# 138 unread bfloat16 products on TensorE in the first part of an attention and two-MLP kernel

## The chip, the cores and the metric

The kernel runs on one core of one Trainium2 chip. The metric is the time of one execution in device microseconds; lower is better. A profile is one execution recorded by the hardware profiler: every instruction with its engine, start and duration, and what it waited for. The engines are TensorE (PE, and PEld for its weight loads), VectorE (DVE), ScalarE (ACT), GpSimd (POOL) and SyncE (SP, whose queue issues the loads). [...]

## The reference

All inputs are float32 tensors in the reference; q, k and v have 4 sequences, 8 heads, 576 positions and 64 features. The weights come to the kernel as 64-bit floats.

```
scores = q @ k.T / 8, masked: heads 0-3 see 32 positions back,
         heads 4-7 see every 4th position up to 128 back
x = softmax(scores) @ v                      # -> 2304 tokens x 512
xn = x / rms(x) * rms_g
x = (silu(xn @ w_gate) * (xn @ w_val)) @ w_out    # d_ff 1536
h = x @ w_in2
out = (max(h, 0) + alpha * min(h, 0)) @ w_out2    # d_ff 2048
```

## The kernel before

The kernel keeps all weights in on-chip memory (SBUF), in 70 slots of 128 x 512 words. A weight block is 512 KB of 64-bit floats; there are 36 blocks of the first MLP (12 each of gate, value and output weights, in chunks of 3 and 9 columns of blocks) and 32 of the second. `load_w` (line 205) loads a block on the SP queue. `decode_w` (line 221) turns it, or a pair of blocks, into float32 by three integer instructions on VectorE (lines 231 to 233). `gram_w1` (line 286) multiplies each decoded gate and value block with itself, four bfloat16 products of 128 x 128 that add into a tile of the pool `ps_a` (tag `acc`, three buffers); once a chunk is complete, VectorE reduces the sums (line 298), `over_partitions` (line 327) spreads the result over the partitions with one product against ones (line 333), and `root_scale` makes the scales. Only then can `split_w` (line 400) cut a block of that chunk into two float16 halves (ScalarE at line 404, VectorE at line 409 or ScalarE and GpSimd at 406 and 407). The first chunk hangs on the first 6 blocks, the second on all 24 gate and value blocks.

The attention works in groups of up to 128 queries. Each of the first groups goes through `f_turn` (q and k are transposed on TensorE, line 639, and ScalarE copies them to a slot, line 642), `f_score` (mask products, then float32 score products of 64 rows; VectorE takes the maximum, line 578; ScalarE the exponentials, line 585), `f_turn_p` (line 670), `f_value` and, for every second group at first, a normalization (`a_norm`, line 734; its rows are transposed at line 750). Groups 0 to 3 make the rows of token block 0. The steps stand in a list; each is wrapped in `early`, which puts its instructions 400 places ahead in the order of priority. Between the steps `pump_to` decodes blocks: 8 of them over the first 18 steps, then more. A planner orders each engine's instructions by these priorities and its own estimate of when each is ready; each engine then takes its instructions in that order.

Behind that come the two MLPs by token blocks of 256 or 384 columns: `mm1` (gate and value), `mm2` (output, into `acc` tiles), `mm3` and `mm4` the same for the second MLP. All products of `mm` are at line 97. `ones_1` is a constant tile of ones in bfloat16, set by VectorE at line 136; `head(b)` is the upper bfloat16 half of a decoded block.

Of the kernel before, what the change touches and what calls it, by code (L numbers as in the profile page):

```python
# [8 lines left out]
F32 = mybir.dt.float32  # L9
F16 = mybir.dt.float16  # L10
BF16 = mybir.dt.bfloat16
# [18 lines left out]
def kernel(  # L30
# [19 lines left out]
    KD = DM // 128  # L50
# [14 lines left out]
    ps_a = ps_stack.enter_context(tc.tile_pool(name="ps_a", bufs=3, space=PSUM))  # L65
# [12 lines left out]
    ones_1 = const.tile([128, 128], BF16, name="ones_1")  # L78
# [17 lines left out]
    def mm(o, a, b, start, stop):  # L96
        nc.tensor.matmul(o, a, b, start=start, stop=stop)  # L97

    def psw():
        return ps_w.tile([128, 512], F32, tag="w", name="psw")  # L100
# [7 lines left out]
    def b_o(c):  # L108
        return 3 * c + 2
# [128 lines left out]
    def dec(b):  # L238
        d = dec_at[b]
        return wb[:, d * 512:(d + 1) * 512]  # L240

    def head(b):
        d = dec_at[b]
        return wbb[:, d * 1024:(d + 1) * 1024].rearrange("p (k f t) -> p k f t", f=128, t=2)[:, :, :, 1]
# [15 lines left out]
    def chunk(c):  # L260
        return max(i for i in range(NCH) if ch0[i] <= c)
# [11 lines left out]
    def gram(blocks, sums, dst):  # L273

        g = psw()
        last = len(blocks) - 1
        for n, b in enumerate(blocks):
            for kc in range(KD):
                w = head(b)[:, kc, :]
                if sums:  # L280
                    mm(g[:, 0:128], w, w, n + kc == 0, n == last and kc == KD - 1)
                else:
                    mm(g[:, n * 128:(n + 1) * 128], w, w, kc == 0, kc == KD - 1)
        nc.vector.tensor_reduce(dst, g[:, 0:128 if sums else (last + 1) * 128], axis=AX.X, op=ALU.max)  # L284

    gsum = {}

# [16 lines left out]
    def norm_w(b):  # L304
        if b < NW1:
            ch = chunk(b // 3)
            if b % 3 < 2:
                gram_w1(b)
            elif b == b_o(ch0[ch + 1] - 1):
                gram([b_o(c) for c in range(ch0[ch], ch0[ch + 1])], True, sqo[:, ch:ch + 1])  # L310
        else:

            n, p = (b - NW1) // 2, (b - NW1) % 2
            junk = wk.tile([128, 512], BF16, tag="junk", bufs=1, name="junk")
            nc.scalar.activation(junk, dec(b), ACTF.Square, accum_out=sq2[:, p, n:n + 1])
            if b == NBLK - 1:
                g = psw()
                sb = const.tile([128, 2], F32, name="sb")
                nc.vector.tensor_reduce(sb, sq2, axis=AX.X, op=ALU.add)
                mm(g[:, 0:2], ones_1, eps[:, 0:2], True, False)  # L320
                mm(g[:, 0:2], ones_1, sb.bitcast(BF16).rearrange("p (n t) -> p n t", t=2)[:, :, 1], False, True)
                nc.vector.tensor_copy(sb2, g[:, 0:2])
# [118 lines left out]
    groups = []  # L441
# [177 lines left out]
    def drop(g, name):  # L619
        for i in g["slots"].pop(name):  # L620
            give(i)
# [9 lines left out]
    def f_turn(i):  # L631
        g = groups[i]
        nq, nk = g["nq"], g["nk"]
        ps = psw().rearrange("p (a c) -> p a c", c=128)
        qk = f32_slot(g, "qk").rearrange("p (a c) -> p a c", c=128)
        g["qk"] = qk
        for u, m in ((0, nq), (1, nk)):
            for a in range(2):
                nc.tensor.transpose(  # L639
                    ps[:, 2 * u + a, :m], g["rqk"][:m, u, 2 * a:2 * a + 2, :].rearrange("p h d -> p (h d)"), ident[:m, :m])  # L640
        if nq == nk:
            nc.scalar.activation(qk[:, :, :nq], ps[:, :, :nq], ACTF.Copy)
        else:
            nc.scalar.activation(qk[:, 0:2, :nq], ps[:, 0:2, :nq], ACTF.Copy)
            nc.scalar.activation(qk[:, 2:4, :nk], ps[:, 2:4, :nk], ACTF.Copy)
        drop(g, "rqk")
# [155 lines left out]

    def turn(i):
        f_turn(i)
        if i >= 3:
            next_load(i)

# [91 lines left out]
    acc = {}  # L899
# [300 lines left out]
    n_done = [0]  # L1200
# [6 lines left out]
    def pump(n):  # L1207

        for _ in range(n):
            if made or loaded:  # L1210
                if made:
                    b = made.popleft()
                else:
                    b = loaded.popleft()

                    if loaded and n_done[0] >= ALONE and abs(raw_at[b] - raw_at[loaded[0]]) == 2 and can_load():
                        pairs[0] += 1
                        made.append(loaded.popleft())
                    decode_w(b, *made)
                norm_w(b)  # L1220
                n_done[0] += 1
                if b == b_o(C1 - 1):
                    scale_wo()
                if b == NBLK - 1:
                    scale_w2()
            fill()
# [32 lines left out]
    fill()  # L1259
    nc.sync.dma_start(out=al, in_=alpha.rearrange("(c p) -> p c", p=128))  # L1260
    constants()

    first = max(n for n, s in enumerate(steps) if s[1] == 0) + 1
    for n in range(first):
# [7 lines left out]
    for s in slots:  # L1272
        kind, j, c = s
# [42 lines left out]
    for n in range(len(order) + 1):  # L1316
        if n < len(order):
            t, cp = order[n]
# [8 lines left out]
        while behind and (n == len(order) or len(behind) > LAGT + (behind[0][1] == 0 < behind[0][0])):  # L1327
            t, cp = behind.popleft()
# [39 lines left out]
```

## Time and profile before

| | |
|---|---|
| three runs | 954.87, 955.4 and 956.1 us; median 955.4 us |
| profiled execution | span 953.2 us from its first to its last instruction; no other time is given for it |
| instructions | 18826, of which TensorE 6760 products |
| TensorE busy | 907.5 us (95%) |
| VectorE busy | 624.7 us (66%) |
| ScalarE busy | 549.1 us (58%) |
| GpSimd busy | 319.1 us (33%) |
| mean granted clock | 0.981 |

Busy time is the time in which at least one instruction of the engine runs. A wait is put down to the instruction that released it. Times in the rows are microseconds from the start of the span.

### The profile page before, as it was taken

Reading aid. Unit: us, or ns where it says so; the run is one execution under the profiler, and the core shown is the slowest. Engines: PE = TensorE matmul, PEld = TensorE weight load, DVE = VectorE, ACT = ScalarE, POOL = GpSimd, SP = SyncE. Lnnn points to the kernel's source line nnn. Section 1 sums busy time; section 2 is a strip of 40 time slices with the busy share of each in tenths; the row PEclk is TensorE's granted clock in tenths of the full one; section 3 lists DMA queues with packets and bytes.
Section 4 is the critical chain, followed back from the end, with each engine's and each line's share of the span. In section 5 each row is a group of like instructions: output and inputs, shape, how many; then the busy total and the mean of one; then the engine's idle time right before and its main releaser. Section 6 shows DMA issues by size and latency. Waiting matters only on the chain.

```text
span 953.2 us, 18826 instructions
## 1 busy us (share of the span) xinstructions
PE 907.5 (95%) x6760; PEld 621.2 (65%) x6760; DVE 624.7 (66%) x1569; ACT 549.1 (58%) x1541; POOL 319.1 (33%) x324
## 2 busy tenths in 40 slices
PE   6668799999999999999999999999999999999997
PEld 4656676775556676555555555555775558889986
DVE  4999997999777555554664765344545837576564
ACT  3436587766799967767665777544524324443342
POOL 2222441131345544332433233232252622322221
PEclk9678999999999999999999999999999999999999
DMA  9992446555435554544454653322301001000000
GB/s 252 327 353 89 120 132 187 144 159 138 86 70 107 97 108 74 123 86 100 102 88 74 114 105 70 65 64 42 55 14 23 1 1 35 1 24 17 9 24 23
DMA packets 191613, 88.14 MB, mean 92 GB/s; under 512 B 176800, under 2 KB 180384, under 8 KB 191520
## 3 DMA queue, kind: packets, MB, share of 16 engines
q1 hardware_dynamic: 189504, 83.27, 37.8%
q10 hardware_dynamic: 2016, 3.67, 1.1%
q8 instruction: 53, 0.87, 0.4%
q14 instruction: 40, 0.33, 0.1%
HBM read 55.32 MB, written 6.55 MB: 65 GB/s over the span
## 4 chain that ended last, share of the span: by engine, by line
PE 83%; DVE 9%; DMA 3%; issue 2%; ACT 1%; SPq 1%; POOL 0%; DVEq 0%; ACTq 0%; POOLq 0%
PE psw L97 41%; PE acc L97 24%; PE p L97 16%; DVE wb L232 2%; DVE wb L233 1%; DVE wb L231 1%; DVE wb L409 1%; DMA wb<-in_moe_w_out_dram 1%; PE psw L670 1%; PE psw L639 1%; SPq L629 1%; DMA wb<-in_q_dram 1%; DVE t L921 1%; DVE t L922 0%; DMA rkv<-in_k_dram 0%
## 5 line engine op out<-in xcount | busy, mean ns | idle before, releaser
L97 PEld LDWEIGHTS <-wb 128*128 128x128 f16 (+1 forms) x4866 | 452.3, 98 | 196.1 <-DVE wb L233 16.7
L97 PE MATMUL psw<-xyall,wb 128*128 128x384 f16 (+1 forms) x2784 | 425.2, 303 | 2.8 <-DVE sqo L284 1.2
L97 PE MATMUL acc<-wb,hlall 128*128 128x512 f16 x822 | 197.6, 379 | 0.2 <-POOL hlall L930 0.2
L97 PEld LDWEIGHTS <-hlall 128*128 128x128 f16 x822 | 79.4, 98 | 79.8 <-POOL hlall L930 0.7
L930 POOL TENSOR_TENSOR hlall<-t,hlall 128x384 f16<-128x384 f32 (+1 forms) x58 | 58.4, 1006 | 150.0 <-ACT hlall L924 132.2
L97 PE MATMUL acc<-wb 128*128 128x512 f16 (+1 forms) x402 | 83.3, 354 | 13.9 <-DVE wb L233 13.9
L97 PE MATMUL p<-xyall,wb 128*128 128x256 f16 (+1 forms) x960 | 88.7, 251 | 0.0
L1098 POOL TENSOR_TENSOR wb<-fa,wb 128x640 f16<-128x640 f32 x32 | 45.4, 1420 | 112.0 <-ACT wb L1097 108.2
L97 PE MATMUL p<-wb 128*128 128x256 f16 x672 | 77.6, 273 | 0.0
L920 ACT ACTIVATE t<-psw,tsc 128x384 f32<-128x384 f32 (+1 forms) x84 | 44.1, 525 | 55.4 <-PE psw L97 54.3
L921 DVE SCALAR_TENSOR_TENSOR t<-t,psw 128x384 f32<-128x384 f32 (+1 forms) x84 | 41.0, 489 | 48.0 <-ACT t L920 48.0
L589 ACT ACTIVATE s<-s,mx 96x128 f32<-96x128 f32 (+2 forms) x132 | 50.1, 380 | 20.9 <-DVE mx L581 20.1
L404 ACT ACTIVATE wb<-wb,wsg 128x512 f16<-128x512 f32 x68 | 46.3, 711 | 16.9 <-DVE wsg L341 10.2
L705 POOL TENSOR_TENSOR phl<-s,phl 96x512 f16<-96x512 f32 (+2 forms) x33 | 35.8, 1084 | 58.2 <-ACT phl L699 41.0
L930 POOL TENSOR_TENSOR hlall<-p,hlall 128x256 f16<-128x256 f32 (+1 forms) x49 | 39.3, 803 | 44.5 <-ACT hlall L987 41.3
L985 DVE SCALAR_TENSOR_TENSOR p<-m,oma,psw 128x256 f32<-128x256 f32 (+1 forms) x64 | 34.7, 542 | 26.7 <-ACT m L984 25.4
L407 POOL TENSOR_TENSOR wb<-wb 128x512 f16<-128x512 f32 x28 | 37.3, 1337 | 41.6 <-ACT wb L406 15.8
L930 POOL TENSOR_TENSOR wb<-t,wb 128x256 f16<-128x256 f32 (+1 forms) x26 | 27.2, 1046 | 70.3 <-ACT wb L924 70.3
L233 DVE SCALAR_TENSOR_TENSOR wb<-wb 128x512 int32<-128x512 int32 (+1 forms) x56 | 49.7, 890 | 0.3
L924 ACT ACTIVATE hlall<-t 128x384 f16<-128x384 f32 (+1 forms) x58 | 27.7, 477 | 37.8 <-DVE t L922 37.8
L737 POOL TENSOR_TENSOR ms<-ms,mhalf 96x1 f32<-96x1 f32 (+2 forms) x24 | 17.2, 718 | 96.2 <-DVE ms L736 84.5
L922 DVE SCALAR_TENSOR_TENSOR t<-t,psw 128x384 f32<-128x384 f32 (+1 forms) x84 | 41.0, 488 | 11.4 <-PE psw L97 10.1
(203 smaller groups left out, 1317.0 us busy)
## 6 DMA issues: line engine op xcount, KB each, us to landing
wb<-in_moe_w_out_dram SPq DMA_DIRECT2D x28, 512.0 KB, 4.6
wb<-in_moe_w_in_dram SPq DMA_DIRECT2D x16, 512.0 KB, 3.8
wb<-in_moe_w_gate_dram SPq DMA_DIRECT2D x12, 512.0 KB, 6.7
wb<-in_moe_w_val_dram SPq DMA_DIRECT2D x12, 512.0 KB, 6.7
out_dram<-o ACTq DMA_DIRECT2D x14, 256.0 KB, 2.7
rkv<-in_k_dram SPq DMA_DIRECT2D x23, 128.0 KB, 2.6
rkv<-in_v_dram SPq DMA_DIRECT2D x23, 128.0 KB, 2.7
rq<-in_q_dram SPq DMA_DIRECT2D x23, 96.0 KB, 2.2
```

What stands on the lines that cost most here:

```text
L97: nc.tensor.matmul(o, a, b, start=start, stop=stop)
L233: nc.vector.scalar_tensor_tensor(w, r[:, :, :, 0], 29, w, ALU.logical_shift_right, ALU.bitwise_or)
L404: nc.scalar.activation(half(b, 0), dec(b), ACTF.Copy, scale=wsg[:, s:s + 1])
L407: nc.gpsimd.tensor_tensor(half(b, 1), dec(b), half(b, 0), ALU.subtract)
L589: nc.scalar.activation(s[:nq, h, :nk], s[:nq, h, :nk], ACTF.Exp, bias=mx[:nq, 1, h:h + 1], scale=-1.0, accum_out=g["dn"][:nq, h])
L705: nc.gpsimd.tensor_tensor(phl[:nq, 1, :, :nk], g["s"][:nq, :, :nk], phl[:nq, 0, :, :nk], ALU.subtract)
L920: nc.scalar.activation(t[:, :T], pg[:, :T], ACTF.Tanh, scale=tsc[:, chunk(c):chunk(c) + 1])
L921: nc.vector.scalar_tensor_tensor(t[:, :T], t[:, :T], 1.0, pg[:, :T], ALU.add, ALU.mult)
L922: nc.vector.scalar_tensor_tensor(t[:, :T], t[:, :T], 2.0 ** -46, pv[:, :T], ALU.mult, ALU.mult)
L930: nc.gpsimd.tensor_tensor(a[:, 1, :T], t[:, :T], a[:, 0, :T], ALU.subtract)
L985: nc.vector.scalar_tensor_tensor(p[:, :T], m[:, :T], oma[:, c:c + 1], ps[:, :T], ALU.mult, ALU.add)
L1098: nc.gpsimd.tensor_tensor(l[:, 3:8], f[:, 3:8], h[:, 3:8], ALU.subtract)
```

## The change

Three places get products whose results nobody reads. All write one tile `hot` of 128 x 512 float32, which is taken from the pool `ps_a` ahead of all its other tiles. The moving operand is always `ones_1`, read four times over (512 columns); the stationary one is `ones_1` itself (10 products, behind the constants and ahead of the first step), the upper bfloat16 half of q and k as `f_turn` left them (8 products in each of turns 0 to 3), or the four parts of a decoded block (4 products for each of the first 24 decoded blocks, behind its Gram products).

```diff
+    HEAT, HEATED = 10, 24
+    hot = ps_a.tile([128, 4, 128], F32, tag="acc", name="hot")
+
+    def heat(w):
+
+        mm(hot, w, ones_1.unsqueeze(1).to_broadcast([128, 4, 128]), True, True)
+
     gsum = {}
...
     def turn(i):
         f_turn(i)
+        if i < 4:
+            qk = groups[i]["qk"].rearrange("p a c -> p (a c)").bitcast(BF16).rearrange("p (a c t) -> p a c t", a=4, t=2)
+            for n in range(8):
+                heat(qk[:, n % 4, :, 1])
         if i >= 3:
             next_load(i)
...
                 norm_w(b)
+                for kc in range(KD if n_done[0] < HEATED else 0):
+                    heat(head(b)[:, kc, :])
                 n_done[0] += 1
...
     constants()
+    for _ in range(HEAT):
+        heat(ones_1)
```

## Rows read from the trace of the kernel before

**Rows 1.** The page: busy tenths of two engines and granted clock, 40 equal slices.

```profile
PE   6668799999999999999999999999999999999997
DVE  4999997999777555554664765344545837576564
PEclk9678999999999999999999999999999999999999
```

**Rows 2.** Engines by stage: length, busy us and instructions of each engine, clock, DMA.

```profile
5.43:14.65 9.22, 5.78 (x25) 3.00 (x25) 4.82 (x9) 1.79 (x3) 2.19 (x6) 1.00 1.16 283
14.65:31.40 16.75, 16.72 (x89) 13.62 (x88) 12.48 (x42) 8.56 (x37) 0.00 (x0) 1.00 1.05 283
31.40:50.40 19.00, 11.36 (x62) 9.83 (x62) 18.68 (x36) 8.74 (x16) 7.65 (x4) 0.55 1.01 342
50.40:64.00 13.60, 10.82 (x100) 8.97 (x100) 13.60 (x23) 4.06 (x13) 1.55 (x1) 1.00 1.03 411
64.00:77.70 13.70, 6.24 (x44) 4.77 (x42) 12.63 (x29) 4.00 (x13) 2.14 (x2) 0.50 0.67 208
77.70:104.20 26.50, 23.28 (x207) 19.90 (x205) 26.46 (x45) 18.15 (x47) 10.56 (x8) 1.00 0.33 99
104.20:117.00 12.80, 8.03 (x74) 6.91 (x74) 11.53 (x23) 7.77 (x17) 7.08 (x7) 0.87 0.32 101
```

**Rows 3.** Mask products by shape, in 14:24 and 50.5:63.5: busy us, mean ns, idle before.

```profile
L97 PE MATMUL psw<-m_spp,ident 128*128 128x256 bf16 x4 | 1.6, 412 | 0.0
L97 PE MATMUL psw<-m_spp,ident 128*128 128x256 bf16 x2 | 0.6, 278 | 0.0
```

**Rows 4.** TensorE's timeline: start, duration, instruction and count, idle before and its releaser.

```profile
4.58 0.28 PE L97 MATMUL psw<-et 4*128 4x128 bf16 x1 [4.58 <-POOL et L149]
5.43 1.30 PE L639 MATMUL psw<-ident,wb 128*128 128x128 f32 x4 [0.57 <-DMA wb<-in_q_dram]
...
12.12 0.61 PE L97 MATMUL acc<-wb 128*128 128x128 bf16 x4 [0.26 <-DVE wb L233]
...
29.84 0.41 PE L97 MATMUL acc<-wb 128*128 128x128 bf16 x4
...
63.78 0.88 PE L97 MATMUL acc<-wb 128*128 128x128 bf16 x8 [2.14 <-DVE wb L233]
70.69 1.89 PE L97 MATMUL acc<-wb 128*128 128x128 bf16 x16 [6.03 <-DVE wb L233]
74.01 0.39 PE L97 MATMUL psw<-diag,ones 128*128 128x256 bf16 x1 [1.43 <-DVE diag L331]
...
74.41 0.64 PE L97 MATMUL psw<-m_spp,ident 128*128 128x256 bf16 x2
74.84 0.42 PE L97 MATMUL psw<-m_spd,ident 128*128 128x256 bf16 x1
...
82.62 0.62 PE L97 MATMUL psw<-wb 128*128 128x128 bf16 x8 [1.69 <-ACT wb L585]
```

**Rows 5.** TensorE in stretches of 0.1 us: length, busy us, clock, DMA.

```profile
63.90:64.00 0.10, 0.10 (x4) 0.95 0.91 369
...
77.60:77.70 0.10, 0.10 (x2) 0.79 0.00 0
```

**Rows 6.** TensorE's timeline, products of 512 columns.

```profile
135.62 5.99 PE L97 MATMUL acc<-wb 128*128 128x512 f16 x27
```

**Rows 7.** VectorE's waits in 0:110: total us, times, longest.

```profile
DVE mx L578 <- PE psw L97: 3.6, 5, 1.3
```

**Rows 8.** VectorE's timeline, columns as in rows 4.

```profile
15.91 0.76 DVE L578 TENSOR_REDUCE mx<-psw 128x2 f32<-128x256 f32 x2 [1.04 <-PE psw L97]
...
25.37 0.40 DVE L231 TENSOR_SCALAR wb<-wb 128x512 int32<-128x512 int32 x1
...
73.03 0.41 DVE L298 TENSOR_REDUCE tmp<-acc 128x2 f32<-128x256 f32 x1
```

**Rows 9.** The SP queue's timeline: issue of block 4's load.

```profile
18.11 0.42 SPq L212 DMA_DIRECT2D wb<-in_moe_w_gate_dram  x1
```

**Rows 10.** DMA issues in 0:80: count, KB each, median us to landing.

```profile
wb<-in_moe_w_gate_dram SPq DMA_DIRECT2D x12, 512.0 KB, 6.7
```

## The prediction, made before the change was run

> **What bounds the kernel now.** I read the 40 slices of the page first, then the engines by stage, then the timelines of TensorE and VectorE in the first 120 us, because all 138 added products lie there. The slices [rows 1] show TensorE at nine tenths or more from the sixth slice (119 us) to the end, and short of it only before, while VectorE is full from the second slice on. By stage [rows 2], VectorE is busy 12.48 of 16.75 us in 14.65 to 31.40, then 18.68 of 19.00, 13.60 of 13.60, 12.63 of 13.70, 26.46 of 26.50 and 11.53 of 12.80. So up to 117 us VectorE (decoding the weights, splitting them, the attention's small steps) is the limit, and TensorE waits for it; behind that TensorE has work without a gap. The work behind 117 us is not touched. The end therefore moves by what the change does to VectorE's idle time before 117 us, or to TensorE's stalls just ahead of that point, and by nothing else.
>
> The clock is the second thing to see. [...] Two such products back to back take 0.64 us where one takes 0.42 [rows 4], so 0.22 us for each further 256 columns, which makes an estimate of 0.43 us for 512 columns. Four Gram products took 0.61 us at 12.12 and 0.41 us at 29.84 [rows 4], so the rise came between; the granted clock later falls at 33.3, rises at 50.4, falls at 64.0, rises at 77.7 and falls again at 108.3 (two of the five shown [rows 5]). At the high level 27 products of 512 columns took 5.99 us, 0.22 us each [rows 6].
>
> **The change part by part.** It removes nothing, adds no DMA and no instruction on any engine but TensorE: 138 products with their weight loads, 10 + 4 x 8 + 24 x 4. At 0.22 us that is 30.4 us, at 0.43 us 59.3 us. Their tile takes one of the three buffers that the accumulators rotate through. The first block's two accumulators then meet it and that of the first chunk's Gram sums, both long done; I cost that at nothing. The slots of turned q and k and of decoded blocks get one more reader, in each case ahead of or beside readers that they have already: nothing, too.
>
> *Ten products ahead of all else.* They need only a constant that VectorE sets at about 1.1 us. TensorE's first product starts at 4.58 us and its first transpose at 5.43 [rows 4]. Ten at 0.43 us end at about 5.4. Cost 0, covered by the wait for the first q and k; without that cover 4.3 us.
>
> *Twenty-four products of turns 0 to 2 and eight of blocks 0 and 1, in 5.43 to 14.65.* At the high level 32 x 0.22 = 7.0 us. TensorE is idle there for 9.22 - 5.78 = 3.44 us [rows 2], and its 5.78 busy us, now at the low level, would give back half, 2.9. The first score comes 0.7 us late.
>
> *From the first score to the last, 14.65 to 24.8.* All of it is at the low level; at the high one it gives back half of 10.2 us, 5.1. The eight products of turn 3 cost 1.8 us. The eight of blocks 2 and 3 would cost 1.8 more if they stood ahead of the scores. The attention's steps are put 400 places ahead in the planner's order and the pump's products are not, so I let those eight fall behind. The last score then ends 0.7 + 1.8 - 5.1 = 2.6 us earlier (0.8 with the eight ahead). VectorE's five waits for score products sum to 3.6 us [rows 7], one of 1.04 us ahead of the first maximum, which stays [rows 8]. What is left, 2.6 us, is as much as the scores gain: I take -2.6. Its bounds are 0 and all 4.27 idle us of that stretch [rows 2]. VectorE can't use the time for decoding, since block 4 is decoded only at 25.37 us [rows 8] and its load takes 6.7 us from an issue at 18.11 [rows 9, 10]; it can use it for the attention steps that now lie behind that point.
>
> *Blocks 4 to 19, 31 to 64 us.* VectorE's waits for TensorE hardly occur here. TensorE is idle 7.64 and 2.78 us in the two stretches from 31.40 to 64.00 [rows 2], and most of the first is at the low level. About 56 products at 0.22 us (12.3 us) fit into 10.4 idle us and some 5 given back. Cost 0; without this cover, 2.
>
> *Blocks 20 to 23, from 70.69.* Here the products are in the way. TensorE waits until 70.69 for the last decoded blocks, makes 16 Gram products in 1.89 us, and VectorE reduces them at 73.03; one product at 74.01 spreads the result, and the scales of the remaining 18 gate and value blocks hang on it [rows 4, 8]. Twelve added products stand ahead of the last block's Gram. At the high level these are 2.6 us, and the Gram products give back 0.9: they end at 74.3 rather than 72.6, where VectorE is ready at 73.03. That is 1.3 us late, of which I let other decoding cover half: +0.7. At the low level (1.89 + 12 x 0.43, ending at 77.7) it is 4.7; with a rise in the middle about 3. I take the high level, because the added products of blocks 16 to 21 shorten the pause ahead of them, but the rows speak against it nearly as much: the clock fell at 64.0 after a pause of 2.14 us [rows 4, 5]. [...]
>
> *74 to 77.7.* Now at the low level throughout; the products before raise the clock sooner. Half of 3.7 us is 1.8, of which ScalarE's exponentials, whose wait stops TensorE for 1.69 us ahead of 82.62 [rows 4], pass on about -1.0 (0 to -1.8).
>
> *104 to 117.* TensorE idles 4.77 us [rows 2] for VectorE's normalized rows and runs slowly from 108.4 on; no added product is left by then: 0.
>
> Sum: -2.6 + 0.7 - 1.0 = -2.9 us. The profiled span is 953.2 us and the median of the runs 955.4, so 2.2 us lie outside the span; the span becomes 950.3 and the time **952.5 us**.
>
> **The rivals.**
>
> *Slower: the products run at the low level ahead of the first score.* Before 29.8 us even gap-free work stayed slow [rows 2, 3], so dense products may stay slow too. Then 32 x 0.43 = 13.8 us meet 3.44 idle us, and the first score, and all behind it, comes 10.3 us late; VectorE waits for it, less about 3 us of its idle time that decoding takes up: 955.4 + 7 = **962.4**. It decides from about 0.3 us a product on, where the delay of the first score eats what the scores give back. Against it: the slow stretch is made of products that use 64 rows or f32 operands, and no row shows bfloat16 products of 128 rows and 512 columns. Chance 0.20.
>
> *No change: the clock falls in the pause before the last four blocks.* TensorE has no more products from block 19's to the decoding of the last blocks, up to 4 us. Falling as at 64.0 [rows 5], it begins the 16 Gram and 12 added products slowly, +3.0 in place of +0.7, and the -1.0 is kept: **954.8**. Chance 0.19.
>
> *No change: VectorE's waits stay.* The exponentials on ScalarE and block 4's arrival set the pace before 25 us, the freed time goes to waiting for them, and the first term is 0: 955.4 + 0.7 - 1.0 = **955.1**. For it: transfers from 2 to 60 us leave the queues hardly a gap. Against it: the waits name the score products [rows 7]. Chance 0.12.
>
> *Much faster: the stall ahead of 117 us goes as well.* The second four attention groups come early by as much as the first, and the 4.77 us of idle time with 1.7 us of low clock vanish: 952.5 - 6.5 = **946.0**. Against it: VectorE is full from 77.7 to 104.2 [rows 2], so those steps have no room to move in. Chance 0.13.
>
> **How the numbers follow.** The forecast has 0.36. A change of 0.2%, 1.9 us, is about what a measurement of this kernel can tell from none. Faster: forecast, last rival and a little of the falling clock, 0.51. Same: most of the two in the middle, 0.22. Slower: the first rival, and 0.07 of the others, since a planner that gets 138 more instructions may order other work worse; 0.27. The forecast's own range is 950 to 953.5. To leave out no more than 0.2 the range reaches to 945.5 (the stall gone) and to 961.5, just short of the full price of the slow products, of which half is thus held.
>
> **What would show it.** Right: mask products at 14 to 24 us at 278 ns, not 412; VectorE's waits for scores near 1 us in sum; the first score within 1 us of 14.65; the last decoded block's reduction at 71 to 72 us, not 73.03; VectorE without gaps up to a point 2 to 4 us earlier. Wrong: added products at 0.43 us behind 6 us; the product of 74.01 later than now; another order of VectorE's decoding with new waits. The forecast fails if the clock is not raised by the first ten, or if other work waits in TensorE's queue behind products that nobody reads.

## The result and the profile after

The changed kernel took 961.71 us (median of four runs, 960.6 to 964.44), the kernel before beside it 955.75 (954.87 to 957.1): a ratio of 1.0065, 95% interval 1.0045 to 1.0084. It is about 6 us slower. The forecast was 952.5, faster; the time lies just above the range, which ends at 961.5. The profiled execution took 961.12 us with a span of 958.9, against 953.2 before, so 5.7 us are to be found.

First the page of the changed kernel, the busy tenths and the granted clock (the profile's share of full speed that TensorE was given, in tenths) in 40 slices, as in [rows 1].

```profile
PE   8898699999999999999999999999999999999997
DVE  4999987999777655654656665344455736666564
PEclk9989799999999999999999999999999999999999
```

TensorE is fuller in the first four slices (8898, 6668 before), and the low clock of the second to the fourth is nearly gone (989, 678 before). In the fifth slice, from 96 to 120 us, both fell: TensorE from 7 to 6, the clock from 9 to 7. VectorE's digits differ little; the stages, with the bounds and columns of [rows 2], say where it lost.

```profile
5.43:14.65 9.22, 7.78 (x45) 4.12 (x45) 4.87 (x9) 1.80 (x3) 2.15 (x7) 1.00 1.18 292
14.65:31.40 16.75, 16.75 (x117) 11.19 (x116) 10.45 (x38) 8.58 (x37) 0.00 (x0) 1.00 1.06 277
31.40:50.40 19.00, 14.85 (x100) 9.53 (x99) 18.69 (x40) 8.46 (x17) 4.57 (x4) 0.91 0.98 327
50.40:64.00 13.60, 11.22 (x67) 7.39 (x66) 12.66 (x17) 3.01 (x12) 0.93 (x1) 0.75 0.99 387
64.00:77.70 13.70, 12.89 (x99) 7.77 (x98) 12.49 (x23) 2.76 (x11) 2.94 (x2) 1.00 0.67 216
...
104.20:117.00 12.80, 4.44 (x27) 3.56 (x25) 12.80 (x22) 6.87 (x14) 6.27 (x7) 0.65 0.38 111
```

VectorE's busy time fell from 12.48 to 10.45 us in 14.65 to 31.40 and from 13.60 to 12.66 in 50.40 to 64.00. TensorE now has no idle time at all in the first of these. Its timeline, with the columns of [rows 4], shows what fills it.

```profile
1.20 4.45 PE L97 MATMUL hot<-ones 128*128 128x512 bf16 x10 [1.20 <-DVE ones L136]
...
7.11 1.90 PE L97 MATMUL hot<-ones,wb 128*128 128x512 bf16 x8
...
13.17 2.76 PE L97 MATMUL hot<-ones,wb 128*128 128x512 bf16 x12 [0.46 <-ACT wb L649]
15.77 0.27 PE L646 MATMUL psw<-ident,wb 128*128 128x128 f32 x1
15.88 0.27 PE L97 MATMUL psw<-m_spp,ident 128*128 128x256 bf16 x1
...
16.30 0.72 PE L97 MATMUL psw<-wb 64*128 64x128 f32 x8
...
21.50 1.90 PE L97 MATMUL hot<-ones,wb 128*128 128x512 bf16 x8
...
26.21 0.49 PE L97 MATMUL psw<-wb 64*128 64x128 f32 x2
...
73.92 0.40 PE L97 MATMUL acc<-wb 128*128 128x128 bf16 x4 [0.81 <-DVE wb L233]
74.16 1.02 PE L97 MATMUL hot<-ones,wb 128*128 128x512 bf16 x4
...
77.21 0.39 PE L97 MATMUL acc<-wb 128*128 128x128 bf16 x4
...
110.33 1.08 PE L757 MATMUL psw<-ident,wb 128*128 128x128 f32 x4 [4.77 <-DVE wb L745]
115.00 1.11 PE L757 MATMUL psw<-ident,wb 128*128 128x128 f32 x4 [3.59 <-DVE wb L745]
```

The clock did rise: a group of eight products takes 1.90 us from 7.11 on, and a mask product 0.27 us at 15.88, where it took 412 ns [rows 3]. The granted clock does not show this: it reads 1.00 from 5.43 to 31.40 us in both kernels. But twelve unread products stand directly ahead of the last transposes and of the first score (13.17), and sixteen more between the first score and the last, eight of them in one row (21.50). The first score starts at 16.30, 1.65 us later than before, and the last one ends at 26.70, where it ended at 24.85. The same places in the kernel before, with the transposes of the two normalized rows at 106 and 109 us:

```profile
14.65 1.23 PE L97 MATMUL psw<-wb 64*128 64x128 f32 x8
...
23.63 1.22 PE L97 MATMUL psw<-wb 64*128 64x128 f32 x4
...
106.10 0.63 PE L750 MATMUL psw<-ident,wb 128*128 128x128 f32 x4 [1.91 <-DVE wb L738]
108.76 1.09 PE L750 MATMUL psw<-ident,wb 128*128 128x128 f32 x4 [2.03 <-DVE wb L738]
```

VectorE's waits in 0 to 110 us (columns of [rows 7]) and its timeline show who pays.

```profile
DVE mx L585 <- PE psw L97: 7.6, 7, 2.5
DVE tmp L305 <- PE acc L97: 0.8, 1, 0.8
```

```profile
17.04 0.76 DVE L585 TENSOR_REDUCE mx<-psw 128x2 f32<-128x256 f32 x2 [2.47 <-PE psw L97]
...
24.19 0.43 DVE L585 TENSOR_REDUCE mx<-psw 128x2 f32<-128x256 f32 x1 [1.87 <-PE psw L97]
...
60.62 0.42 DVE L585 TENSOR_REDUCE mx<-psw 128x2 f32<-128x256 f32 x1 [0.94 <-PE psw L97]
...
77.64 0.43 DVE L305 TENSOR_REDUCE tmp<-acc 128x2 f32<-128x256 f32 x1 [0.77 <-PE acc L97]
```

The waits for scores are 7.6 us in seven places; they were 3.6 in five [rows 7]. The reduction of the second chunk's Gram sums is at 77.64 instead of 73.03 [rows 8]. That reduction is the first of three points between which the 5.7 us can be divided, by the VectorE timelines of both kernels:

| from | to | before | after | difference |
|---|---|---|---|---|
| start | reduction of the second chunk | 73.03 | 77.64 | +4.61 |
| that reduction | second normalized row behind it (L738, now L745) | 34.84 | 35.92 | +1.08 |
| that row | reduction of the square sums (L284) | 8.08 | 8.79 | +0.71 |
| that reduction | end of the span | 837.25 | 836.55 | -0.70 |

Of the first 4.61 us, 3.90 are idle time of VectorE (16.99 us ahead of the reduction, 13.09 before). The remaining 0.7 is not more work: the same 131 instructions stand ahead of it in both kernels, and they take 60.65 us instead of 59.93. In the second line VectorE has other work: 69 instructions instead of 64, busy 1.6 us longer and idle 0.5 us less. The five stand behind the row in the kernel before. The third line has a longer low clock in it: the clock fell at 108.1 us (108.4 before), but in 1-us stretches (columns of [rows 2]) it is low until 118.3 us, where it was low until 111.8 before.

```profile
108.00:109.00 1.00, 0.00 (x0) 0.00 (x0) 1.00 (x1) 0.33 (x2) 0.10 (x1) 0.54 0.00 0
...
118.00:119.00 1.00, 1.00 (x10) 0.82 (x8) 0.85 (x2) 0.00 (x0) 0.00 (x0) 0.84 1.00 227
```

### The profile page after: what moved, and what is told of

Read it like the earlier page. It is cut to its first block, busy times and chain, and to the rows that moved or that the text cites. A ratio compares the mean times of both kernels' runs of the same rounds, so it can differ in the third digit from the quotient of the medians.

```text
span 958.9 us, 19102 instructions
## 1 busy us (share of the span) xinstructions
PE 927.3 (97%) x6898; PEld 624.9 (65%) x6898; DVE 626.4 (65%) x1569; ACT 548.5 (57%) x1541; POOL 316.3 (33%) x324
## 4 chain that ended last, share of the span: by engine, by line
PE 78%; DVE 9%; issue 4%; ACT 4%; DMA 3%; POOL 1%; SPq 0%; DVEq 0%; POOLq 0%; ACTq 0%
PE psw L97 36%; PE acc L97 22%; PE p L97 16%; PE hot L97 2%; DVE wb L232 1%; ACT wb L411 1%; DVE wb L233 1%; DMA wb<-in_moe_w_out_dram 1%; DVE wb L231 1%; DVE wb L416 1%; PE psw L646 1%; ACT s L596 1%; DVE t L933 1%; DMA rkv<-in_k_dram 1%; ACT wb L413 1%
## 5 line engine op out<-in xcount | busy, mean ns | idle before, releaser
L97 PEld LDWEIGHTS <-wb 128*128 128x128 f16 (+1 forms) x4994 | 462.4, 98 | 202.1 <-DVE wb L233 10.4
L932 DVE SCALAR_TENSOR_TENSOR t<-t,psw 128x384 f32<-128x384 f32 (+1 forms) x84 | 41.1, 489 | 48.4 <-ACT t L931 48.3
L996 DVE SCALAR_TENSOR_TENSOR p<-m,oma,psw 128x256 f32<-128x256 f32 (+1 forms) x64 | 34.7, 542 | 26.7 <-ACT m L995 25.3
L233 DVE SCALAR_TENSOR_TENSOR wb<-wb 128x512 int32<-128x512 int32 (+1 forms) x56 | 48.7, 873 | 0.3
L232 DVE SCALAR_TENSOR_TENSOR wb<-wb 128x512 int32<-128x512 int32 (+1 forms) x56 | 48.6, 872 | 0.2
```

The source lines that it names most:

```text
L232: nc.vector.scalar_tensor_tensor(w, r[:, :, :, 1], -0x40000000, w, ALU.bitwise_and, ALU.bitwise_or)
L233: nc.vector.scalar_tensor_tensor(w, r[:, :, :, 0], 29, w, ALU.logical_shift_right, ALU.bitwise_or)
L932: nc.vector.scalar_tensor_tensor(t[:, :T], t[:, :T], 1.0, pg[:, :T], ALU.add, ALU.mult)
L996: nc.vector.scalar_tensor_tensor(p[:, :T], m[:, :T], oma[:, c:c + 1], ps[:, :T], ALU.mult, ALU.add)
```

## The experiments

Three theories stood when they began. **Theory A, the queue:** score and Gram products that VectorE waits for stand behind products that nobody reads, as the first score at 16.30 does behind the twelve of 13.17; what a place costs depends on who waits there, and grows with the columns. **Theory B, the thing itself:** the tile that takes a turn among three buffers, or the earlier rise and later fall of the clock, costs the time wherever the products are. **Theory C, the order:** 138 more instructions lead the planner to another order of VectorE's work, and that order is worse whatever TensorE does.

All edits are against the changed kernel; all ratios are against the kernel before, timed on the same chip. The table has, from the profiled run of each, VectorE's idle time ahead of the second chunk's reduction, the start of that reduction, the time from it to the second normalized row behind it, the start of the square sums' reduction, and the span.

| run | unread products | ratio, 95% interval | idle | reduction | to row | squares | span |
|---|---|---|---|---|---|---|---|
| before | 0 | 1 | 13.09 | 73.03 | 34.84 | 115.95 | 953.2 |
| after | 138 | 1.0065, 1.0045 to 1.0084 | 16.99 | 77.64 | 35.92 | 122.35 | 958.9 |
| e1_first10 | 10 | 0.9992, 0.9976 to 1.0008 | 13.37 | 73.39 | 34.85 | 116.27 | 953.0 |
| e4_one | 1 | 0.9994, 0.9979 to 1.0009 | 13.60 | 73.69 | 34.85 | 116.65 | 955.2 |
| e2_first_and_turns | 10 + 32 | 1.0002, 0.9984 to 1.0020 | 14.05 | 74.18 | 34.71 | 118.44 | 956.7 |
| e16_first_two | 10 + 16 | 1.0000, 0.9987 to 1.0014 | 11.59 | 71.51 | 35.15 | 116.56 | 953.2 |
| e13_narrow_turns | 10 + 32 narrow | 1.0081, 1.0057 to 1.0105 | 14.26 | 74.93 | 35.29 | 119.24 | 955.9 |
| e23_first_eight | 10 + 32 at blocks 0 to 7 | 1.0020, 1.0006 to 1.0034 | 14.83 | 75.31 | 34.85 | 119.25 | 955.6 |
| e10_mid | 48 at blocks 8 to 19 | 1.0008, 0.9996 to 1.0019 | 13.53 | 73.88 | 34.87 | 117.94 | 953.9 |
| e22_last_four | 16 at blocks 20 to 23 | 1.0049, 1.0030 to 1.0068 | 14.82 | 74.69 | 35.93 | 120.00 | 956.0 |
| e11_behind | 16 behind block 19 | 1.0006, 0.9990 to 1.0021 | 13.20 | 72.29 | 35.03 | 116.77 | 953.4 |
| e3_blocks | 96 at blocks 0 to 23 | 1.0035, 1.0020 to 1.0050 | 18.44 | 78.73 | 35.92 | 122.57 | 958.0 |
| e6_to20 | 122, none at 20 to 23 | 1.0038, 1.0024 to 1.0051 | 14.78 | 74.76 | 35.03 | 117.79 | 956.4 |
| e15_two_turns | 122, none in turns 2, 3 | 1.0058, 1.0043 to 1.0074 | 17.56 | 77.84 | 35.92 | 122.07 | 962.4 |
| e18_two_turns_to20 | 106, neither of both | 1.0011, 0.9998 to 1.0025 | 12.23 | 72.43 | 34.91 | 116.83 | 955.7 |
| e12_double_turns | 170 | 1.0083, 1.0058 to 1.0108 | 18.40 | 78.84 | 35.94 | 124.80 | 963.8 |
| e5_narrow | 138 narrow | 1.0023, 1.0008 to 1.0037 | 11.75 | 72.37 | 35.91 | 117.13 | 956.2 |

The ratios are not the quotients of the medians in the text, which can differ from them by up to 0.002 (e2). One execution of the kernel before can take 953.2 to 960.95 us, and the part behind the squares' reduction scatters between the profiles (835.4 to 840.3 us), so the span of one profile decides little. The profiled execution is also not always a middle one: it is the shortest of six in e13 and e22, and the longest of six in e15.

**The first ten alone, and one alone.**

```diff
-    HEAT, HEATED = 10, 24
+    HEAT, HEATED = 10, 0
...
-        if i < 4:
+        if i < 0:
```

> Only the ten products ahead of all else; every engine keeps the order of the kernel before. Theory A (the added products cost because other products queue behind them on TensorE, more than the raised clock gives back): nothing queues here, the clock rises near 6 us as with the full change; if it holds through part of the scores, VectorE's waits for scores shrink from 3.6 us towards 2 and the time is 1 to 3 us below before; if it falls in the pauses up to 14 us, no difference. Theory B (the cost is the raised clock's or the tile's, for example a buffer of the accumulators lost): slower, 957 to 960. Theory C (the planner's new order is the whole cost): no loss, as the order is kept; 953 to 956.

Neither cost nor gain: 956.15 us beside 956.28. Its TensorE timeline tells why there is no gain.

```profile
5.79 0.84 PE L646 MATMUL psw<-ident,wb 128*128 128x128 f32 x4
...
11.27 1.23 PE L646 MATMUL psw<-ident,wb 128*128 128x128 f32 x4 [3.18 <-DMA wb<-in_q_dram]
...
14.34 0.42 PE L97 MATMUL psw<-m_spp,ident 128*128 128x256 bf16 x1
```

The clock rose (0.84 us for four transposes, 1.30 before [rows 4]) and fell again in the wait of 3.18 us for q: the transposes behind it take 1.23, the mask product 0.42.

```diff
-    HEAT, HEATED = 10, 24
+    HEAT, HEATED = 1, 0
...
-        if i < 4:
+        if i < 0:
```

> The tile and one product ahead of all else; every engine keeps the order of the kernel before. All theories but one: no difference, 954.5 to 957. If the accumulators' buffer that the tile takes costs anything, this kernel shows it: over 957.

One product, with the tile and its buffer, costs nothing (956.4 us): theory B has lost its tile.

**The turns without the blocks.**

```diff
-    HEAT, HEATED = 10, 24
+    HEAT, HEATED = 10, 0
```

> The ten first products and the 32 of the turns, none behind the decoded blocks. Theory A: the first score starts near 16.3 us as with the full change, the last ends about 1 us later than before or no later, block 4 is decoded at 25.5 to 26.5 us; 955 to 958. Theory C (order): anything from 952 to 962 by what order the planner makes; a loss that no wait on TensorE explains.

No difference that can be measured, though the reduction is 1.15 us later and block 4 is decoded only at 27.73 us. The medians are 958.22 and 956.28 us, and the interval of the ratio reaches to 1.0020, so a loss of 1 to 2 us here is not excluded.

```diff
-    HEAT, HEATED = 10, 24
+    HEAT, HEATED = 10, 0
...
-        if i < 4:
+        if i < 2:
```

> The ten first products and the 16 of turns 0 and 1, where TensorE waits for q and k anyway; nothing else. Theory A: the clock is high for at least the first scores and nothing is delayed: block 4 decoded at 25 us, the second chunk's reduction at 72 to 73 us; 954.5 to 956 where before is near 956. If even this is slower, the raised clock is worth less than the planner's scatter.

Without the products of turns 2 and 3 the first part does what was forecast on TensorE: the first score is at 13.87 us, the last one ends at 20.23, VectorE waits for no score at all, block 4 is decoded at 23.68 instead of 25.37 [rows 8], and the reduction comes 1.52 us early. But VectorE now waits for ScalarE's exponentials (columns of [rows 7]; e16 first, then the kernel before), so that it is busy only 0.89 us more in 14.65 to 31.40 (13.37 us, 12.48 before).

```profile
DVE dn L603 <- ACT wb L592: 2.5, 2, 1.3
```

```profile
DVE dn L596 <- ACT wb L585: 0.4, 1, 0.4
```

The time is still that of before. Its TensorE timeline, and the clock in one 1-us stretch, show where the 1.5 us went.

```profile
13.87 0.72 PE L97 MATMUL psw<-wb 64*128 64x128 f32 x8
...
104.36 0.63 PE L757 MATMUL psw<-ident,wb 128*128 128x128 f32 x4 [2.59 <-DVE wb L745]
107.97 1.09 PE L757 MATMUL psw<-ident,wb 128*128 128x128 f32 x4 [2.98 <-DVE wb L745]
...
109.81 4.65 PE L97 MATMUL psw<-xyall,wb 128*128 128x256 f16 x23
```

```profile
107.00:108.00 1.00, 0.03 (x1) 0.07 (x1) 1.00 (x2) 1.00 (x2) 1.00 (x2) 0.51 0.00 0
```

TensorE waits 2.59 and 2.98 us for the normalized rows (1.91 and 2.03 before), the clock falls at 107.0 and stays low until 113.9, 6.8 us instead of 3.4, and 23 products take 4.65 us where they took 3.26. The squares' reduction is 0.6 us later than before, not 1.5 earlier.

```diff
-    HEAT, HEATED = 10, 24
+    HEAT, HEATED = 10, 0
...
-    def heat(w):
+    def heat(w, n=4):
...
-        mm(hot, w, ones_1.unsqueeze(1).to_broadcast([128, 4, 128]), True, True)
+        mm(hot[:, 0:n], w, ones_1.unsqueeze(1).to_broadcast([128, n, 128]), True, True)
...
-                heat(qk[:, n % 4, :, 1])
+                heat(qk[:, n % 4, :, 1], 1)
```

> The ten first products of 512 columns and the 32 of the turns of 128 columns, none behind blocks. Theory A: the clock is high at the scores and little stands before them; block 4 is decoded at 25.4 us or before, VectorE's waits for scores are 2 to 3 us, the second chunk's reduction is at 72 to 73 us, and the time is that of before or up to 1 us less. Theory C: a loss of 1 to 3 us between that reduction and the last one of the output weights at 116 us, from the new order.

This is the run that no theory explains. Narrow products in the turns should cost less than wide ones; the median is 964.65 us over six runs from 957.8 to 966.41, and the profiled run is the shortest of the six, so that no trace shows what the others lost. In that one the granted clock reads 7577 in the first four slices (9989 in the changed kernel) and 0.68 on average up to the reduction; VectorE waits 2.9 us for scores, and the reduction comes 1.90 us late.

**Blocks without turns.**

```diff
-    HEAT, HEATED = 10, 24
+    HEAT, HEATED = 0, 24
...
-        if i < 4:
+        if i < 0:
```

> Only the 96 products behind the first 24 decoded blocks. Theory A: most of the loss is here, from the products of blocks 2 and 3 between the scores (at the low clock, 0.43 us each) and from those ahead of the last Gram products; the scales of the second chunk 3 to 6 us later than before; 958 to 964. Theory B (the turns' products carry the loss): 955 to 957.

About half of the loss is there without a product in the turns (1.0035, where the full change has 1.0065). VectorE waits 4.05 us for the last Gram product at its reduction, 78.73.

```diff
-    HEAT, HEATED = 10, 24
+    HEAT, HEATED = 0, 20
...
-        if i < 4:
+        if i < 0:
...
-                for kc in range(KD if n_done[0] < HEATED else 0):
+                for kc in range(KD if 8 <= n_done[0] < HEATED else 0):
```

> Only the 48 products behind blocks 8 to 19; the planner keeps VectorE's order but for 25 lines of 1530. Theory A: block 4 is decoded at 25.4 us as before; behind it one or two waits of VectorE for the second four groups' scores or for Gram products, 0.9 to 1.4 us in sum, and the second chunk's reduction later than 73.0 by just that sum; 956 to 958 where before is near 956. Theory C (order): no loss, since the order is nearly kept.

Blocks 8 to 19 alone: 955.82 us beside 955.59, no difference that can be measured, though VectorE waits 0.58 us for the last Gram product and the reduction is 0.86 us later.

```diff
-    HEAT, HEATED = 10, 24
+    HEAT, HEATED = 10, 8
...
-        if i < 4:
+        if i < 0:
```

> The ten first products and the 32 behind the first eight blocks. If the rest of the loss lies here: VectorE waits for scores that stand behind the products of blocks 2 and 3, block 4 is decoded at 26 to 27.5 us, and the time is 1 to 2 us over before. If it lies in the later blocks or in the sum: no difference, 955 to 957.

The ten and blocks 0 to 7: 1.0020, about 2 us, with the reduction 2.28 us late. VectorE's waits for scores are 1.9 us here, less than before, so this loss is for the most part not of the kind that theory A names. Three waits stand in VectorE's timeline ahead of the reduction that the kernel before lacks: 1.05 us at 24.05 for the load of `rms_g`, 1.24 us at 59.31 for ScalarE, and 0.66 us for the last Gram product, the only one of theory A's kind. Why the first two appear stays open.

**The last four blocks.**

```diff
-    HEAT, HEATED = 10, 24
+    HEAT, HEATED = 0, 24
...
-        if i < 4:
+        if i < 0:
...
-                for kc in range(KD if n_done[0] < HEATED else 0):
+                for kc in range(KD if 20 <= n_done[0] < HEATED else 0):
```

> Only the 16 products behind the last four gate and value blocks. Theory A: TensorE has paused before them, so they and the Gram products between them start at the low clock; VectorE waits 2 to 5 us for the last Gram product, the reduction comes at 75 to 78 us in place of 73.0, and about 1 us more is lost behind it, where the full change has the same order of VectorE's steps; 958 to 960 where before is near 956. If these products cost only in company with the others: 955.5 to 957.

Sixteen products, a ninth of all, make 1.0049. The profiled run is the shortest of six (958.26; median 962.41), so its trace shows the mildest case; where the others lost 4 us more, no trace shows. TensorE, and VectorE's reduction:

```profile
69.20 0.61 PE L97 MATMUL acc<-wb 128*128 128x128 bf16 x4 [6.12 <-DVE wb L233]
69.61 1.91 PE L97 MATMUL hot<-ones,wb 128*128 128x512 bf16 x4
...
73.40 1.02 PE L97 MATMUL hot<-ones,wb 128*128 128x512 bf16 x4
```

```profile
74.69 0.42 DVE L305 TENSOR_REDUCE tmp<-acc 128x2 f32<-128x256 f32 x1 [3.07 <-PE acc L97]
```

After a pause of 6.12 us four products take 1.91 us, later 1.02; VectorE waits 3.07 us.

```diff
-    HEAT, HEATED = 10, 24
+    HEAT, HEATED = 0, 24
...
-        if i < 4:
+        if i < 0:
...
-                for kc in range(KD if n_done[0] < HEATED else 0):
-                    heat(head(b)[:, kc, :])
+                for kc in range(16 if n_done[0] == 19 else 0):
+                    heat(head(b)[:, kc % KD, :])
```

> Only 16 products, all behind block 19, in the pause ahead of the last four blocks where TensorE waits 6 us. Theory A: nothing VectorE needs stands behind them, if they end by 70.7 us; the clock stays high through the last Gram products and the scores at 75 to 79 us, which would give back 1 to 2 us: 954 to 956 where before is near 956. If the raised clock is worth nothing at all: no difference. If they end late, the second chunk's reduction is later than 73 us and the time up to 2 us longer.

The same number of products one block earlier, with no Gram product behind them that the reduction waits for. No loss: 1.0006. The 16 Gram products are made in 1.09 us instead of 1.89 [rows 4] and the reduction comes 0.74 us early. But two stretches of 1 us tell what comes next.

```profile
72.00:73.00 1.00, 0.00 (x0) 0.00 (x0) 1.00 (x3) 0.00 (x0) 0.00 (x0) 1.00 0.72 287
73.00:74.00 1.00, 0.26 (x2) 0.20 (x3) 0.69 (x3) 0.00 (x0) 0.00 (x0) 0.54 0.80 160
```

In the wait of 2.10 us for the reduced sums the clock falls, and the scores of 75 to 83 us run at the low level: the granted clock is 0.50 there, and twelve score products take 2.08 us at 74.92, where they take 1.16 in the changed kernel at 79.29.

```diff
-    HEAT, HEATED = 10, 24
+    HEAT, HEATED = 10, 20
```

> The full change without the products behind the last four gate and value blocks (122 in all). Theory A with the last Gram products as main place: the wait of 0.77 us ahead of the reduction and that of 0.38 us ahead of the scales go, and so does what the planner put there; 958 to 960. Theory A with the scores as main place: 960 to 962, about as the full change. Theory C: undetermined.

All but the last sixteen: 1.0038. The row is again 35.03 us behind the reduction, not 35.92. VectorE still waits 6.5 us for scores.

**Both places.**

```diff
-        if i < 4:
+        if i < 2:
```

> The full change without the products of turns 2 and 3 (122 in all). Theory A: the first score comes at 15 us and block 4 is decoded at 25 to 26 us in place of 27.5, so the second chunk's reduction comes 1.5 to 2 us earlier than with the full change, and the time is 2 us below it: 959 to 960. If the first scores' delay is covered by later idle time anyway: as the full change, 961 to 962.5.

```diff
-    HEAT, HEATED = 10, 24
+    HEAT, HEATED = 10, 20
...
-        if i < 4:
+        if i < 2:
```

> The full change without the products of turns 2 and 3 and without those of the last four blocks (106 left). If the loss is the sum of its places: VectorE's waits for TensorE up to the reduction are those of before or fewer, the reduction comes at 73 to 74 us, and the time is 956 to 957.5. If the planner's order by itself costs: 958 to 960, with the difference behind the reduction.

Without the products of turns 2 and 3 alone, the loss hardly changes (1.0058); without these and the last sixteen, it is gone within the uncertainty (1.0011, 0.9998 to 1.0025; 958.39 us beside 956.61). A rest of 1 us or so is not excluded: the reduction comes 0.6 us early in e18 and the squares' reduction 0.9 us late. The trace of e15 is that of the longest of its six executions (964.63 us; the other five 960.23 to 961.98). In it, TensorE and VectorE with the last sixteen:

```profile
71.21 0.61 PE L97 MATMUL acc<-wb 128*128 128x128 bf16 x4 [3.79 <-DVE wb L233]
71.61 1.91 PE L97 MATMUL hot<-ones,wb 128*128 128x512 bf16 x4
...
77.41 0.39 PE L97 MATMUL acc<-wb 128*128 128x128 bf16 x4
```

```profile
77.84 0.42 DVE L305 TENSOR_REDUCE tmp<-acc 128x2 f32<-128x256 f32 x1 [4.82 <-PE acc L97]
```

and TensorE without them (e18):

```profile
70.69 1.10 PE L97 MATMUL acc<-wb 128*128 128x128 bf16 x16 [2.22 <-DVE wb L233]
```

VectorE has decoded the last block at 73.02 us in the first and at 72.5 in the second. In the first it then waits 4.82 us for Gram products that stand between unread ones at the low clock, in the second not at all.

**Size.**

```diff
-            for n in range(8):
+            for n in range(16):
```

> The full change with 16 products in each of turns 0 to 3 in place of 8 (32 more, 7 us at the high clock). Theory A: the first score comes 4 to 6 us later than with the full change, VectorE's waits for scores grow from 7.6 us to 11 or more, and the time by 3 to 6 us: 965 to 968. Theory C: no more than the scatter of another order, 958 to 963.

965.11 us, a little more than the changed kernel; the intervals overlap. The first score is at 18.59. The waits for scores did not grow to the 11 us that theory A asked for (5.8 us in five places, the longest 3.1); block 4 is now decoded ahead of some of them (26.07).

```diff
-        mm(hot, w, ones_1.unsqueeze(1).to_broadcast([128, 4, 128]), True, True)
+        mm(hot[:, 0], w, ones_1, True, True)
```

> All 138 products at their places, each of 128 columns in place of 512. Theory A (VectorE waits for products that stand behind the added ones on TensorE): the added TensorE time falls to about a third, the sum of VectorE's waits for scores falls from 7.6 us towards 4, the wait ahead of the second chunk's reduction is under 0.5 us, and most of the 6 us goes: 955 to 958. Theory C (the planner's new order costs, not the products' time): the planner orders VectorE's work about as differently from before as with the full change, so the loss stays, 959 to 963.

A quarter of the columns in all 138 products: 1.0023 instead of 1.0065, between what the two theories asked for. Waits for scores are 2.0 us, and the reduction comes even 0.66 us early. What is left of the loss lies behind it: 35.91 us to the second row, and the clock low from 102.9 to 113.2 and from 120.0 to 123.4 us. VectorE's idle time ahead of the squares' reduction is that of before (15.06 us, 15.04 before); the 1.18 us by which that comes late are the same 207 instructions, which take 102.08 us here instead of 100.91.

**What follows for the theories.** Theory A holds for most. In the changed kernel VectorE's waits for scores and for the last Gram product are 8.4 us where they were 3.6, and its other waits shrank a little. In all runs the reduction moves with VectorE's idle time ahead of it: +3.9 idle and +4.6 us in the changed kernel, +5.35 and +5.7 in e3, +1.7 and +1.7 in e6, +5.3 and +5.8 in e12, -1.5 and -1.5 in e16. That by itself is little more than arithmetic, since about the same instructions stand ahead of the reduction in every run; what the idle time waits for has to be read from the waits, and in e23 and e16 it is not TensorE for the most part. Columns count (1.0023 in e5, 1.0065 with four times as many). Theory B fell for the tile (e4; e11, which writes it until 67.7 us, costs nothing either) and for the early rise of the clock by itself (e1, e16). Theory C holds for about 1 us: the stretch from the reduction to the second row is 35.9 us in all six kernels with products behind each of the last four blocks, narrow ones included, and 34.7 to 35.3 in all others. The counts show the order itself: in those six kernels 69 instructions of VectorE stand in that stretch and 7 between the row and the squares' reduction, in the others 64 to 67 and 9 to 12; up to the squares' reduction there are 207 in every one. What this order costs at the end of the span is not shown by a run with the order alone. No version was faster than the kernel before.

## Why the prediction was wrong

**The failing step is "From the first score to the last":** -2.6 us predicted, +2.0 measured (VectorE's busy time in 14.65 to 31.40 is 2.03 less). That is 4.6 of the 8.6 us between the predicted sum, -2.9, and the measured one, +5.7. The clock half was right: mask products take 273 ns in 14 to 24 us, as the prediction asked for. What failed most is the placing of the products. Those of blocks 2 and 3 were to fall behind the scores because attention steps have 400 places of priority. By their count in the timeline, 28 products stand ahead of the first score (three turns and one block) and 16 between the first and the last (turn 3 and two blocks); only one block's four fall behind. The prediction had 1.8 us for turn 3's eight, and 0.8 for the step if eight more stood ahead. The rest of the miss is the clock's share: in e16, with none of the sixteen, the scores take from 13.87 to 20.23, 6.36 us instead of 10.20 (the first eight products 0.72 us instead of 1.23, which is more than half), so the clock gives back 3.8 us and not 5.1. Together: +1.65 for the first score, some +3.5 for sixteen products at 0.22 us, -3.8; that is +1.35 of the 1.85 us by which the last score ends later. The remaining 0.5 is about one group of four transposes of the next step (0.66 us at 25.63), which now stands ahead of the last score. So of the 4.45 us between the end of the last score as predicted (2.6 earlier) and as measured (1.85 later), eight more products between the scores make 1.7, the clock's smaller share 1.3, the later first score 0.95 and that group 0.5. The step failed in a second place, too: with the products out of the way and the last score 4.6 us earlier (e16), VectorE gains 0.89 us in that stretch and not what the scores gain, because it waits 2.5 us for the exponentials. In part that is what the rival "VectorE's waits stay" said.

**Ahead of the first score**, +0.7 was right in kind and too small, 1.65. The sum let 32 products fill all of TensorE's 3.44 idle us and what the clock gave back. But a turn's products can't start before ScalarE has copied that turn's q and k, so TensorE still waits 0.69 and 0.46 us for the copies, and turn 2's become ready just when the last transposes do: the twelve at 13.17 delay the first score from 13.87 (e16) to 16.30, 2.4 us.

**The first ten:** 0 predicted, 0 measured (e1). They end at 5.65, where the estimate was about 5.4: ten products of 512 columns take 4.45 us, 0.45 each, and the estimate of 0.43 was worked out from mask products of 256 columns, 0.64 us for two and 0.42 for one [rows 4].

**Blocks 4 to 19:** 0 predicted. In the changed kernel the scores at 59 us wait behind a group of products at the low clock (57.46 to 59.16, four in 1.91 us; 1.02 at 66.63), and VectorE is idle 0.94 us there and 0.41 us at 65.95: +1.35. Alone, blocks 8 to 19 cost nothing measurable (e10), so here the place costs only together with the rest; with which part of it, no run isolates.

**The last four blocks:** +0.7 predicted, with +3.0 for a clock that falls and 4.7 for a clock that stays low. The wait at the reduction is 0.77 us in the changed kernel, which looks like a hit, and isn't. Sixteen products here alone cost 1.0049 (e22). In the changed kernel VectorE's decoding itself ends only at 76.87 instead of 73.10, because of 3.1 us more idle time ahead and 0.7 us more for the same instructions, and TensorE, busy without a pause from 66.40 to 73.11, still has a granted clock of 1.00 at 73.92 and makes the 28 products in 3.7 us. Take the early delay away (e15): VectorE is ready at 73.02, TensorE has paused 3.79 us, the 28 products take 6.6 us, nearly all at the low level (0.50 from 71 to 77 us), and the reduction is at 77.84 again. So in this execution two costs meet at one point, and removing one uncovers the other. It is the longest of six; that the other five lose their time (the ratio is 1.0058) in the same place is not shown. The rival of the falling clock had this mechanism, and the size of its low-level bound (4.7; e15 waits 4.8), as a small loss on top of a gain that did not come. A slow start behind a pause is what e15 and e22 show (3.79 and 6.12 us, then 1.91 us for four unread products, 1.02 later); in the changed kernel itself the pause there was 0.81 us, and the four behind it took 1.02.

**74 to 77.7, and the stall ahead of 117:** -1.0 and 0 predicted, +1.8 measured (+1.08 and +0.71). TensorE's waits for the normalized rows grew from 1.91 and 2.03 us to 4.77 and 3.59. The gain at 74 to 77.7 could not come, since the scores there start 4.1 us later (79.29 instead of 75.19). The rival of 946.0, in which this stall goes, went the other way: even where the reduction came early (e16, e11), the clock then fell in TensorE's waits further on and stayed low for 6.8 us, not 3.4.

**The rivals and the sum.** The slower rival, 962.4, gave nearly the right time by the wrong mechanism: behind the first ten the products ran at 0.23 to 0.24 us ahead of the first score, not at 0.43. What the prediction named last, "other work waits in TensorE's queue behind products that nobody reads", is what happened. The sum as measured: +3.9 of VectorE's idle time and +0.7 for the same instructions taking longer up to the reduction, +1.1, +0.7 and -0.7 behind it, +5.7. The sum of the prediction had no term for another order of VectorE's work, the +1.1; a worse order stood there only in a chance, the 0.07 that "slower" got beside its rival.

**What stays open:** the scatter of e13, e12, e15 and e22 over six runs (4 to 9 us) and the loss of e13 with it, and what the order of theory C costs by itself. In part the scatter goes with the clock: in e15 the longest execution has a mean granted clock of 0.985, the other five 0.989 to 0.991; in e12 the two at 961 to 962 us have 0.992, the four from 964.6 us up 0.986 to 0.988. In e13 and e22 the mean clock does not tell the executions apart.

## What to carry to other kernels

In the clearest places here, products that nobody reads cost what VectorE waited for the product behind them, not their own time: the first ten take 4.45 us and cost nothing (e1), the twelve at 13.17 take 2.76 us, and VectorE's wait ahead of its first maximum is 2.47 us instead of 1.04. Ask of each place which product comes next and who waits for it, and take the order from the planner's result, not from its priorities. A higher clock ahead of a wait was worth nothing where it fell again in the next wait (e1, 3.18 us; e11, 2.10 us); look for the last wait on the way to the bound before counting what the clock gives back. Two costs that meet at one point need not add, so take them out together as well as one by one: of the loss of 0.65%, e6 takes away 0.27, e15 0.07 and e18, which does both, 0.54. The intervals of the four ratios are too wide to show by themselves that this is more than the sum; the trace of e15 is what shows how it can be.

## What the runs showed of the hardware

In the kernel before the granted clock reads 0.50 from 65 to 77 us and 1.00 from 78 to 82. At 0.50 a mask product takes 0.42 us, four transposes of a normalized row 1.09 and four unread products of 512 columns 1.91; at 1.00 these take 0.27 (before, 74.84 and 78.06), 0.63 (before, 108.76 and 106.10) and 1.02 us (e22, 69.61 and 73.40). Up to 31.40 us the granted clock tells nothing of this: it reads 1.00 while the ten take 4.45 us. The time at which the products of the first 33 us got faster differed between two executions: in the kernel before, mask products still took 412 ns on average up to 24 us [rows 3]; in e22, which adds nothing ahead of block 20, they took 0.42 us at 14.18 and 0.27 at 18.29, with scores, masks, transposes and Gram products without a gap in between. So "gap-free work stayed slow" in the prediction was one execution's reading. In the changed kernel the four transposes right behind the ten bfloat16 products of 512 columns took 0.66 us at 5.76, not 1.30 [rows 4]. And in these runs the length of a pause alone did not say whether the clock fell in it: it fell in a wait of 2.10 us in e11 (to 0.50 by 74 us), and after one of 2.22 us in e18 sixteen Gram products still took 1.10 us at 1.00 (1.89 in the kernel before [rows 4]).
